# Block-sparse attention and a rational feed-forward layer on one core: the first two groups of input weights scaled and split through TensorE, loaded in pairs

## The chip, the core and the metric

One core of one Trainium2 chip runs the whole kernel. Time is device microseconds (us) for one execution. TensorE is PE in the profile, with its weight load PEld; VectorE is DVE, ScalarE is ACT, GpSimd is POOL, and SyncE, which issues most of the loads and stores, is SP.

## What is computed

Attention over blocks of 32 positions, 4 batches of 8 heads, 768 positions, 64 values per head; its output goes row by row through a feed-forward layer whose activation is a quotient of two polynomials. The feed-forward weights come as 64-bit floats.

```python
scores = scale * np.matmul(q, k.transpose(0, 1, 3, 2))
# kept: neighbouring blocks, first and last block, and 3 sampled blocks for each block of queries
scores = np.where(mask, scores, -1000000000.0)
attn = softmax(scores)
x = (attn @ v) as 3072 rows of 512

h = x @ w_in                      # 512 x 2048
P = a[0] + a[1] * h + a[2] * h**2 + a[3] * h**3
Q = 1.0 + abs(b[0]) * abs(h) + abs(b[1]) * h**2
out = (P / (Q + 1e-06)) @ w_out   # 2048 x 512
```

## The kernel before

The 3072 rows are 12 chunks of 256. For each chunk attention makes `x` (32 rows at a time, `attention`), splits it in two f16 parts `xh` and `xl`, and then eight **units** (`unit`, of 256 hidden values each) run: 24 matmuls into a PSUM tile `ph` (L1036 to L1038, `into`), three ScalarE passes and seven VectorE passes that make the quotient as `gh` (L1071) and its rest `gl` (L1081), and three groups of four matmuls into `acc` (L1093, L1095, L1099). The two `ph` buffers are one ring, `r_ph`.

Before the units can run, the weights have to be decoded (`weights`, L390 on). **w_in** is 4 column groups `u` of 512 columns, each of 4 row pieces `x` of 128 rows. A piece of 64-bit words (512 KB) is loaded into memory that `wo_l` and `wo_b` will use later. `convert` (L154 by DVE or POOL, L150 by ACT) scales the high word, and three VectorE operations L441, L444, L447 (`pack1` to `pack3`) shift and join the bits into a 32-bit float in place. `most` (L378, ACT) takes the largest absolute value of each piece. When the four pieces of a group are done, `w_scaled` finds one power of two for each group (`scales`: a transpose on TensorE, L339, and small VectorE operations L344 to L356, then L502), and for each piece runs three operations: `scaled` (L154, times the power of two, into a scratch tile `dw`, a ring of three), `high` (L150, to f16), and `low` (L519, POOL, the rest as f16). **w_out** is 16 pieces, each converted, packed and split in the same way into `wo_h`, `wo_l` and `wo_b`, with the same `dw` ring and a ring of two load buffers `wl`.

Each group's scale and the scale of the batch's `v` make the factors that the unit multiplies by (`factors`, L1010): four tiny VectorE operations for each group of the first batch, and four for each later batch.

What sets the order: nothing is issued as it is written. Every step is an `Op` with an engine (or a choice among engines, `among`), a price in ns, the steps it follows, a priority, and the ring buffers it takes. `issue` is a list scheduler that plays these forward and writes the instructions of every engine in the order it found. Where TensorE would idle early on, `fill` (L162) puts in matmuls of the identity whose result nobody reads. A step that may run on several engines goes to the one where it could start first, with the home engine preferred:

```python
key = (max(t - slack, now[e]) + (0 if e == o.engs[0] else other[e]), o.prio, o.n)
```

Of the kernel before, what the change touches and what calls it, by code (L numbers as in the profile page):

```python
# [11 lines left out]
F32 = mybir.dt.float32  # L12
# [3 lines left out]
I32 = mybir.dt.int32  # L16
# [8 lines left out]
def kernel(  # L25
# [68 lines left out]
    nc.vector.tensor_copy(out=ident16, in_=ident)  # L94

# [19 lines left out]
    class Op:  # L115


        def __init__(self, eng, price, run, after=(), prio=0.0, takes=(), uses=(), unit=None, behind=None):
# [9 lines left out]
            self.next, self.at, self.work = [], dict.fromkeys(self.engs, 0.0), 1.0  # L128
# [35 lines left out]
    def issue(ahead):  # L164
# [13 lines left out]
        busy, window, warm = {}, 0, False  # L178
        for n, o in enumerate(plan):
# [9 lines left out]
        fsh = 0.8  # L189
        other = {VE: 500, SC: 534.0, PO: 243.0}  # L190
        unit_of = {VE: nc.vector, SC: nc.scalar, PO: nc.gpsimd}
        slack, fend, f00, fgap = 21.0, 80000, 3000, 0
        while left:
# [53 lines left out]
            else:  # L247
                end = t = t + price
# [40 lines left out]
    absb = const.tile([P, 2], F32, name="absb")  # L289
    bias = const.tile([P, NB, NS], F32, name="bias")  # L290
# [6 lines left out]
    def setup():  # L297
        nc.vector.tensor_scalar(out=ix, in0=samp[0:1].rearrange("p i (n w) -> p i n w", w=2)[:, :, :, 0],
                                scalar1=0, scalar2=NB - 1, op0=ALU.max, op1=ALU.min)
        nc.scalar.activation(out=absb, in_=par[:, 4:6], func=AF.Abs)  # L300

# [66 lines left out]
    scrap = const.tile([P, 512], F16, name="scrap")  # L368
# [7 lines left out]
    def bound(src, mx):  # L376

        nc.scalar.activation(out=scrap[:, :src.free_size()], in_=src, func=AF.Abs, accum_out=mx)  # L378
# [18 lines left out]
    def weights():  # L397
# [5 lines left out]
        for u in range(NG):  # L403
            pieces += [(min(place[0, 2 * u], place[1, 2 * u]) + -4.91, 0, u, x) for x in range(NCC)]
# [5 lines left out]
        def raw(u, x):  # L410
            x0 = (x // 2 if u == 0 else 2 + x // 2) * NCC
            home = [wo_l, wo_b][x % 2][:, x0:x0 + NCC]
            return home.rearrange("p a n -> p (a n)").bitcast(I32)

        def homes(x):
            x //= NCC
            return [freed[0 if x < 2 else NG - 1, 2 * (x % 2) + y] for y in range(2)]

        def one(prio, kind, u, x, before):
# [4 lines left out]
            def load():  # L424
# [5 lines left out]
                if u == 0 and x == 0:  # L430
                    nc.gpsimd.tensor_copy(out=d["ld"][:, 0:1].bitcast(F32), in_=kall[:, 12, 0, 0:1])
                (nc.sync if u > 1 else nc.gpsimd).dma_start(out=d["ld"], in_=wi64[r0:r0 + P, u * 2 * WC:(u + 1) * 2 * WC])

            def convert(eng):
                d["w"] = early.tile([P, WC], I32, name="dw", bufs=3) if kind else wi[:, x, u].rearrange("p a n -> p (a n)").bitcast(I32)
                d["words"] = d["ld"].rearrange("p (n w) -> p n w", w=2)
                times(eng, d["w"].bitcast(F32), d["words"][:, :, 1].bitcast(F32), 2.0 ** -112)
# [5 lines left out]
            def pack2():  # L443
                nc.vector.scalar_tensor_tensor(out=d["w"], in0=d["words"][:, :, 0], scalar=29, in1=d["w"], op0=ALU.logical_shift_right, op1=ALU.bitwise_or)  # L444

            def pack3():
                nc.vector.scalar_tensor_tensor(out=d["w"], in0=d["words"][:, :, 1], scalar=-2 ** 31, in1=d["w"], op0=ALU.bitwise_and, op1=ALU.bitwise_or)  # L447

            def most():
                if u not in sums:  # L450
                    sums[u] = early.tile([P, 8], F32, name="sums")
                bound(d["w"].bitcast(F32), sums[u][:, x:x + 1])
# [9 lines left out]

            wl = [s_wl] if kind else []
            if kind or u > 1:
                o0 = Op(SY, [(475, 524288)], load, [o_setup] if kind else [freed[u - 1, x]], prio - 2, takes=wl, behind=before[kind])
            else:
                o0 = Op(PO, [(700, 524288)], load, [k_evac[0][3]] if u == 0 else [begun[0, x]], -17.0 + 1.2 * x if u else -84, behind=before[kind])
# [5 lines left out]
            o = Op(VE, 335, pack1, [o], prio, uses=w)  # L473
            o = Op(VE, 602, pack2, [o], prio, uses=wl + w)
            o = Op(VE, 602, pack3, [o], prio, uses=wl + w)
# [770 lines left out]
```

## Time and profile before

| what | value |
|---|---|
| median of 3 runs | 829.0 us (827.88 to 829.31) |
| profiled execution, its own time | 828.6 us |
| its span in the profile | 826.8 us |
| busy: PE, PEld, DVE, ACT, POOL | 770.6, 557.3, 674.9, 569.7, 107.5 us |
| instructions in the span | 27468 |
| POOL's last busy slice of 40 | slice 11 (all later ones are 0) |

The profiled execution's own time is 1.8 us over its span. A row of a view of instructions gives the start, the duration, engine, line and tiles; a group's row gives the total, the mean duration of one in ns and, behind the second bar, the idle time of the engine just before them with what ended it. The granted clock (PEclk) is a share of TensorE's full 2.4 GHz; 0.50 is the lower level, 1.2 GHz.

### The profile page before, as it was taken

How to read it: one execution, taken by the hardware profiler on the slowest of the kernel's cores; microseconds unless marked ns; L12 is line 12 of the kernel's file. 1: busy time of each engine (PE TensorE's matmuls, PEld its weight loads, DVE VectorE, ACT ScalarE, POOL GpSimd, SP SyncE). 2: the span in 40 equal slices, each digit the busy share in tenths (PEclk: the TensorE clock that was granted, in tenths of full speed). 3: DMA queues.
4: the chain of work that ended last, by engine and by line, in shares of the span. 5: the costliest groups of instructions: out<-in, count | busy, mean ns of one | idle time of the engine just before them, and what ended most of it. 6: DMA issues, size and time to landing. Idle time of an engine off the chain costs nothing.

```text
span 826.8 us, 27468 instructions
## 1 busy us (share of the span) xinstructions
PE 770.6 (93%) x10859; PEld 557.3 (67%) x10943; DVE 674.9 (82%) x1580; ACT 569.7 (69%) x1264; POOL 107.5 (13%) x149
## 2 busy tenths in 40 slices
PE   8798918898999999999999999999999999999997
PEld 4556605676677768677777767677777767767774
DVE  2788999899988885788878884887888886887886
ACT  2676777677866769677576759676676758766563
POOL 3547485613100000000000000000000000000000
PEclk9999969899999999999999999999999999999999
DMA  7988874537566957545636757635555436220000
GB/s 210 242 220 238 233 231 138 163 87 189 142 154 165 214 162 194 162 123 162 160 108 164 191 145 196 173 96 157 144 151 149 117 111 182 76 65 2 1 26 26
DMA packets 224416, 121.29 MB, mean 147 GB/s; under 512 B 62624, under 2 KB 214048, under 8 KB 224288
## 3 DMA queue, kind: packets, MB, share of 16 engines
q1 hardware_dynamic: 223136, 115.34, 51.6%
q0 software_dynamic: 1152, 4.19, 1.6%
q8 instruction: 86, 1.41, 0.8%
q14 instruction: 42, 0.34, 0.1%
HBM read 108.47 MB, written 11.01 MB: 145 GB/s over the span
## 4 chain that ended last, share of the span: by engine, by line
PE 81%; DVE 7%; DMA 4%; issue 3%; ACT 2%; POOL 2%; SPq 1%; ACTq 0%; POOLq 0%; DVEq 0%
PE acc L1093 11%; PE ph L1036 9%; PE acc L1095 9%; PE acc L1099 9%; PE ph L1037 9%; PE ph L1038 9%; PE m L817 7%; PE av L940 6%; PE m L894 6%; PE acc L162 3%; DMA vg<-in_v_dram 2%; PE m L556 2%; DMA wl<-in_moe_w_out_dram 1%; PE m L978 1%; POOL wo_h L154 1%
## 5 line engine op out<-in xcount | busy, mean ns | idle before, releaser
L1037 PE MATMUL ph<-xl,wi 128*128 128x256 f16 x768 | 210.5, 274 | 3.1 <-DVE xl L989 3.1
L1036 PE MATMUL ph<-xh,wi 128*128 128x256 f16 x768 | 210.9, 275 | 1.4 <-DVE tt L1053 1.4
L1038 PE MATMUL ph<-xh,wi 128*128 128x256 f16 x768 | 210.7, 274 | 0.0
L1043 ACT ACTIVATE sq<-ph,fc 128x512 f32<-128x512 f32 x96 | 65.9, 687 | 112.6 <-PE ph L1038 112.4
L1093 PE MATMUL acc<-wo_h,gh 128*128 128x512 f32 x384 | 114.5, 420 | 18.7 <-DVE gh L1071 18.0
L848 ACT ACTIVATE pr<-pr,st 128x256 f32<-128x256 f32 x224 | 110.7, 501 | 14.3 <-DVE st L860 14.3
L1060 DVE SCALAR_TENSOR_TENSOR ab<-sq,absb,ab 128x512 f32<-128x512 f32 x96 | 73.2, 763 | 37.1 <-ACT ab L1057 36.9
L829 DVE CUSTOM_DVE_ANT_1 pr<-m,bias 128x256 f32<-128x256 f32 x224 | 83.2, 418 | 22.3 <-PE m L817 22.1
L1099 PE MATMUL acc<-wo_b,gl 128*128 128x512 bf16 x368 | 95.4, 379 | 3.4 <-issue 2.1
L1095 PE MATMUL acc<-wo_l,gh 128*128 128x512 bf16 x316 | 86.5, 384 | 4.6
L1036 PEld LDWEIGHTS <-wi 128*128 128x128 f16 x768 | 75.9, 99 | 21.4 <-issue 5.1
L1071 DVE SCALAR_TENSOR_TENSOR gh<-tt,par,rr 128x512 fp32r<-128x512 f32 x96 | 72.3, 753 | 19.8 <-ACT rr L1067 11.2
L1093 PEld LDWEIGHTS acc<-wo_h,gh 128*128 128x128 f32 x384 | 66.0, 191 | 32.7 <-issue 19.6
L150 ACT ACTIVATE pT<-m 128x512 f32<-128x512 f32 x112 | 64.1, 596 | 34.0 <-PE m L894 32.7
L1037 PEld LDWEIGHTS <-wi 128*128 128x128 f16 x768 | 75.6, 98 | 12.7 <-issue 0.2
L1038 PEld LDWEIGHTS <-wi 128*128 128x128 f16 x768 | 75.5, 98 | 12.6 <-issue 3.4
L1047 ACT ACTIVATE tt<-ph,par,fc 128x512 f32<-128x512 f32 x96 | 74.8, 779 | 0.3 <-DVE gl L1081 0.2
L1050 DVE TENSOR_TENSOR tt<-tt,sq 128x512 f32<-128x512 f32 x96 | 66.9, 697 | 9.4 <-ACT tt L1047 9.4
L1057 ACT ACTIVATE ab<-ph,fc 128x512 f32<-128x512 f32 x96 | 65.6, 683 | 11.2 <-DVE tt L1077 10.5
L1077 DVE SCALAR_TENSOR_TENSOR tt<-tt,par,ab 128x512 f32<-128x512 f32 x96 | 72.2, 752 | 0.5
L894 PE MATMUL m<-ident,pr 128*128 128x128 f32 x448 | 69.6, 288 | 2.9 <-ACT kt L150 2.3
L1053 DVE SCALAR_TENSOR_TENSOR tt<-ph,fc,tt 128x512 f32<-128x512 f32 x96 | 71.4, 744 | 0.8
(130 smaller groups left out, 1221.7 us busy)
## 6 DMA issues: line engine op xcount, KB each, us to landing
vg<-in_v_dram SPq DMA_DIRECT2D x312, 64.0 KB, 2.9
vg<-in_v_dram SPq DMA_DIRECT2D x88, 192.0 KB, 3.6
kall<-ks SPq DMA_DIRECT2D x138, 64.0 KB, 1.9
wl<-in_moe_w_out_dram SPq DMA_DIRECT2D x16, 512.0 KB, 4.8
vg<-in_v_dram SPq DMA_DIRECT2D x12, 512.0 KB, 5.1
kall<-ks SPq DMA_DIRECT2D x23, 256.0 KB, 3.7
ldq<-in_q_dram SPq DMA_DIRECT2D x20, 256.0 KB, 3.4
out_dram<-ld SPq DMA_DIRECT2D x20, 256.0 KB, 2.4
```

The costliest lines, as they stand in the source:

```text
L829: nc.vector.tensor_tensor_reduce(out=prs[x][:, e, g].rearrange("p (s r) -> p s r", r=BLK), in0=h["sp"][g][:, e], in1=add.rearrange("p (s o ...
L848: nc.scalar.activation(out=prs[x][:, e, g], in_=prs[x][:, e, g], func=AF.Exp, scale=SCALE, bias=st[:, 12 + y:13 + y], accum_out=st[:, 16 + ...
L894: nc.tensor.transpose(pp[:, jj * P:(jj + 1) * P], pr[:, e, g, kt:NS * BLK:2], ident)
L1036: nc.tensor.matmul(o, wh, xh[:, :, cc], start=(cc == 0), stop=False)
L1037: nc.tensor.matmul(o, wh, xl[:, :, cc], start=False, stop=False)
L1038: nc.tensor.matmul(o, wl, xh[:, :, cc], start=False, stop=(cc == NCC - 1))
L1047: nc.scalar.activation(out=d["tt"], in_=d["ph"], func=AF.Identity, scale=d["cst"][:, 3:4], bias=par[:, 2:3])
L1060: nc.vector.scalar_tensor_tensor(out=d["ab"], in0=d["sq"], scalar=absb[:, 1:2], in1=d["ab"], op0=ALU.mult, op1=ALU.add)
L1071: nc.vector.scalar_tensor_tensor(out=d["gh"], in0=d["tt"], scalar=par[:, 0:1], in1=d["rr"], op0=ALU.add, op1=ALU.mult)
L1093: nc.tensor.matmul(acc, g, wo_h[:, f], start=(new and e == 0), stop=False)
L1095: nc.tensor.matmul(acc, g, wo_l[:, f], start=False, stop=False)
L1099: nc.tensor.matmul(acc, g, wo_b[:, f], start=False, stop=(last and e == 1))
```

## The change

- **Pairs.** A piece of w_in is now two of the former ones (1 MB for a load): 8 loads, conversions and bounds instead of 16, 24 packing operations instead of 48, each over twice the elements.
- **Groups 0 and 1 through TensorE.** Their scale is put on a diagonal matrix `dg` (one VectorE operation of 128x128 for each group). `whole` is a 32-bit matmul of `dg` with the piece into a `ph` buffer, `high` is ACT's copy of it to f16, `less` subtracts this f16 part in the same buffer by a matmul with a negated identity `minus16`, and `rest` is ACT's copy of what is left. Groups 2 and 3 keep the three operations as they were.
- **Factors.** One VectorE operation over a table of four coefficients (`coefs`, filled at the start) takes the place of four.
- **The scheduler** adds to VectorE's clock a share (`drag`) of the time for which certain POOL steps run beside it, and the prices of two POOL choices for w_out go up (`out_high` 588 to 1050, `out_low` 1225 to 1400).

```diff
-            pieces += [(min(place[0, 2 * u], place[1, 2 * u]) + -4.91, 0, u, x) for x in range(NCC)]
+            pieces += [(min(place[0, 2 * u], place[1, 2 * u]) + -4.91, 0, u, x) for x in range(0, NCC, 2)]
...
-            o = Op(among("c", SC, sc=520, po=588, ve=335), 0, convert, [o0], prio, takes=w, uses=wl)
+            o = Op(among("c", SC, sc=520, po=588, ve=335) if kind else among("c", SC, sc=890, po=1200, ve=602), 0, convert, [o0], prio, takes=w, uses=wl)
+            o.drag = 0.36
...
-                o1 = Op(among("o", SC, sc=520, po=588, ve=335), 0, out_high, [o], prio, uses=w)
-                o2 = Op(among("p", PO, po=1225, ve=602), 0, out_low, [o1] + homes(x), prio, uses=w)
+                o1 = Op(among("o", SC, sc=520, po=1050, ve=335), 0, out_high, [o], prio, uses=w)
+                o2 = Op(among("p", PO, po=1400, ve=602), 0, out_low, [o1] + homes(x), prio, uses=w)
+                o2.drag = 0.62
...
         def keep(s, inv):
+            if u < 2:
+                dg.append(p2.tile([P, P], F32, name="dg"))
+                nc.vector.tensor_scalar(out=dg[0], in0=ident, scalar1=s, scalar2=None, op0=ALU.mult)
...
+                def whole():
+                    d["w"] = ps_h.tile([P, 512], F32, name="ph")
+                    nc.tensor.matmul(d["w"], dg[0], wi[:, x, u].rearrange("p a n -> p (a n)").bitcast(F32), start=True, stop=True)
+
+                def less():
+                    nc.tensor.matmul(d["w"], minus16, wi[:, x, u, 0], start=False, stop=True, skip_group_check=True)
+
+                def rest():
+                    nc.scalar.activation(out=wi[:, x, u, 1], in_=d["w"], func=AF.Copy)
...
+                if u < 2:
+                    a = Op(TE, 880, whole, [o], prio, takes=[s_ws])
+                    a = Op(among("h", SC, sc=520), 0, high, [a], prio, uses=[s_ws])
+                    a = Op(TE, 230, less, [a], prio, uses=[s_ws])
+                    a = Op(SC, 520, rest, [a], prio, uses=[s_ws])
+                else:
+                    a = Op(among("s", PO, po=671, ve=396, sc=613), 0, scaled, [o], prio, takes=[s_ws])
+                    a.drag = 0.36
...
-            for j, coef in enumerate((1.0, absb[:, 0:1], par[:, 1:2], par[:, 3:4])):
-                nc.vector.tensor_scalar(out=fcs[b][:, j, u:u + n], in0=wscale[:, u:u + n], scalar1=v_inv[b], scalar2=coef, op0=ALU.mult, op1=ALU.mult)
+            nc.vector.scalar_tensor_tensor(out=fcs[b][:, :, u:u + n], in0=coefs.rearrange("p (j o) -> p j o", o=1).broadcast_to([P, 4, n]), scalar=v_inv[b],
+                                           in1=wscale[:, u:u + n].rearrange("p (o u) -> p o u", o=1).broadcast_to([P, 4, n]), op0=ALU.mult, op1=ALU.mult)
...
+                if e == PO and o.drag:
+                    while pooled and pooled[0][1] < t - 20000:
+                        pooled.pop(0)
+                    pooled.append((t, t + price, o.drag))
+                    late = o.drag * max(0.0, min(now[VE], t + price) - max(t, last_dve))
+                    now[VE] += late
+                if e == VE:
+                    last_dve = t
+                    price += dragged(t, price)
```

How the order moves, at two places. First VectorE between the scale of group 0 and the second half of chunk 0's `xl` (L1010 before, L1070 after, are the factors; `sums` is the largest value of group 1). Before:

```order
L502 COPY wscale<-scw 128x1 x2
L154 TENSOR_SCALAR dw<-wi,scw 128x512
L663 TENSOR_REDUCE mx<-mx 128x1
...
L660 COPY xscale<-sc_1035 128x1
L1010 TENSOR_SCALAR fc<-wscale,sc_1035 128x2
L1010 TENSOR_SCALAR fc<-wscale,sc_1035,absb 128x2
L1010 TENSOR_SCALAR fc<-wscale,sc_1035,par 128x2 x2
L498 TENSOR_REDUCE sums<-sums 128x1
```

and now:

```order
L721 COPY xscale<-sc_1013 128x1
L1070 SCALAR_TENSOR_TENSOR fc<-coefs,sc_1013,wscale 128x4x2
L535 TENSOR_REDUCE sums<-sums 128x1
L1050 SCALAR_TENSOR_TENSOR xl_120<-m_105,xscale,xh_119 128x512
L1027 TENSOR_TENSOR xn<-av,st 128x256
L468 TENSOR_SCALAR dw<-dw 128x512
L471 SCALAR_TENSOR_TENSOR dw<-wl,dw 128x512
L1050 SCALAR_TENSOR_TENSOR xl_120<-m_104,xscale,xh_119 128x512
L369 TENSOR_REDUCE scw<-m_105 128x1
```

The four factor operations are one, the scaling of a piece is gone from VectorE, `xl` stands directly behind the factors, and the scale of group 1 (`scw`), which stood ahead of the second `xl`, now stands behind it.

Second TensorE ahead of the first unit (L1001 is `av`, L556 here the new `whole`, L559 the new `less`, L164 the fills). Now:

```order
L1001 MATMUL av<-vg_114,pT 32x64 x16
L556 MATMUL ph<-wi,dg 128x512
L955 MATMUL m_104<-ident,pr 128x128 x4
L556 MATMUL ph<-wi,dg 128x512
...
L559 LDWEIGHTS minus_95
L559 MATMUL ph<-wi,minus_95 128x512
...
L556 MATMUL ph<-wi,dg 128x512 x2
L1039 MATMUL m_104<-ident,xn 128x128 x4
L559 LDWEIGHTS minus_95
L559 MATMUL ph<-wi,minus_95 128x512
```

None of these stood there before; fills did. Over the whole kernel the fills go from 135 to 121, and the two blocks of scores (L817) that stood ahead of the first unit's matmuls now stand behind them. From the 25th group of `acc` matmuls on, TensorE's order is the same before and after.

## Rows read from the trace of the kernel before

**Rows 1.** Busy time of the engines in stretches, with granted clock and DMA (columns first).

```profile
core 0: us, PE busy (x) PEld busy (x) DVE busy (x) ACT busy (x) POOL busy (x), PEclk, DMA share, GB/s
...
45.00:75.00 30.00, 27.80 (x574) 18.71 (x572) 27.00 (x75) 22.40 (x58) 20.37 (x27) 1.00 0.77 213
75.00:100.00 25.00, 20.48 (x350) 14.17 (x353) 21.25 (x63) 15.26 (x32) 11.18 (x17) 0.93 0.91 251
100.00:125.00 25.00, 7.38 (x35) 4.60 (x35) 23.23 (x41) 19.38 (x53) 18.77 (x10) 0.69 0.71 219
125.00:160.00 35.00, 27.95 (x583) 21.74 (x582) 32.26 (x73) 25.86 (x59) 23.70 (x28) 0.88 0.52 152
160.00:230.00 70.00, 65.87 (x935) 48.20 (x931) 69.77 (x157) 52.86 (x115) 15.91 (x15) 1.00 0.56 146
230.00:826.80 596.80, 583.60 (x7750) 426.44 (x7821) 476.51 (x1083) 412.88 (x896) 0.00 (x0) 1.00 0.48 130
```

**Rows 2.** What TensorE waited for, 45 to 160 us: total, times, longest.

```profile
PE acc L1093 <- DVE gh L1071: 18.0, 2, 17.6
```

**Rows 3.** Chain of work that ended last, 52 to 158 us: start, duration, what.

```profile
53.07 3.47 DVE fc L1010 x4
...
86.87 6.17 DMA wl<-in_moe_w_out_dram
...
101.42 7.89 POOL wo_h L154
```

**Rows 4.** Groups of VectorE instructions, 0 to 230 us, shapes apart.

```profile
L441 DVE TENSOR_SCALAR wi<-wi 128x512 int32<-128x512 int32 x16 | 7.5, 479 | 0.1
...
L444 DVE SCALAR_TENSOR_TENSOR wi<-wo_l,wi 128x512 int32<-128x512 int32 x8 | 5.5, 689 | 0.1
...
L154 DVE TENSOR_SCALAR dw<-wi,scw 128x512 f32<-128x512 f32 x4 | 4.9, 1239 | 3.4 <-POOL wi L519 2.0 <-POOL wo_l L461 1.4
L1010 DVE TENSOR_SCALAR fc<-wscale,sc,par 128x2 f32<-128x2 f32 x8 | 4.6, 613 | 0.0
...
L1010 DVE TENSOR_SCALAR fc<-wscale,sc 128x2 f32<-128x2 f32 x4 | 2.4, 603 | 0.0
...
L1010 DVE TENSOR_SCALAR fc<-wscale,sc,absb 128x2 f32<-128x2 f32 x4 | 2.0, 506 | 0.0
...
L347 DVE TENSOR_SCALAR scw<-scw 128x1 f32<-128x1 f32 x4 | 0.6, 142 | 0.0
...
L154 DVE TENSOR_SCALAR wi<-wo_b 128x512 f32<-128x512 f32 x1 | 0.4, 397 | 0.0
```

**Rows 5.** Timeline of VectorE, 61 to 73 us: start, duration, what.

```profile
61.99 1.21 DVE L444 SCALAR_TENSOR_TENSOR dw<-wl,dw 128x512 int32<-128x512 int32 x1
63.13 1.13 DVE L860 TENSOR_SCALAR st<-st 128x4 f32<-128x4 f32 x1
...
71.20 1.27 DVE L441 TENSOR_SCALAR dw<-dw 128x512 int32<-128x512 int32 x1
```

**Rows 6.** Groups of GpSimd instructions, 0 to 230 us.

```profile
L519 POOL TENSOR_TENSOR wi<-dw,wi 128x512 f16<-128x512 f32 x16 | 19.6, 1247 | 5.2 <-ACT wi L150 5.2
L154 POOL TENSOR_SCALAR wo_h<-dw 128x512 fp32r<-128x512 f32 x8 | 14.3, 1794 | 37.2 <-DVE dw L447 22.6 <-DVE st L872 8.7 <-DVE st L860 5.9
L154 POOL TENSOR_SCALAR dw<-wi,scw 128x512 f32<-128x512 f32 x12 | 9.6, 805 | 12.7 <-DVE scw L356 11.0 <-DVE wo_l L461 1.4
...
L154 POOL TENSOR_SCALAR wi<-wo_b 128x512 f32<-128x512 f32 x4 | 3.0, 753 | 0.0
```

**Rows 7.** One group of ScalarE instructions, 0 to 230 us.

```profile
L150 ACT ACTIVATE wi<-dw 128x512 f16<-128x512 f32 x16 | 9.8, 625 | 4.7 <-DVE dw L154 2.4 <-POOL dw L154 2.3
```

**Rows 8.** Groups of TensorE instructions, the whole span.

```profile
L1093 PE MATMUL acc<-wo_h,gh 128*128 128x512 f32 x384 | 114.5, 420 | 18.7 <-DVE gh L1071 18.0 <-ACT ld L150 0.7
...
L894 PE MATMUL m<-ident,pr 128*128 128x128 f32 x448 | 69.6, 288 | 2.9 <-ACT kt L150 2.3 <-ACT pT L150 0.6
```

**Rows 9.** Busy time of the fills (L162) alone, 45 to 75 us.

```profile
45.00:75.00 30.00, 12.07 (x51) 4.69 (x49) 1.00 0.77 213
```

More of the change, by code (lines that the diff above doesn't have):

```diff
@@ L94 @@
     nc.vector.tensor_copy(out=ident16, in_=ident)
+    minus16 = const.tile([P, P], F16, name="minus16")
+    nc.vector.tensor_scalar(out=minus16, in0=ident, scalar1=-1.0, scalar2=None, op0=ALU.mult)
     VE, SC, PO, TE, SY = "DVE", "Activation", "Pool", "PE", "SP"
@@ L127, in __init__ @@
                 s.left += 1
-            self.next, self.at, self.work = [], dict.fromkeys(self.engs, 0.0), 1.0
+            self.next, self.at, self.work, self.drag = [], dict.fromkeys(self.engs, 0.0), 1.0, 0.0
             plan.append(self)
@@ L178, in issue, with dragged @@
         busy, window, warm = {}, 0, False
+        pooled = []
+        def dragged(t, price):
+            more = 0.0
+            for a, b, drag in pooled:
+                more += drag * max(0.0, min(b, t + price) - max(a, t))
+            return more
         for n, o in enumerate(plan):
@@ L376, in bound @@
     def bound(src, mx):
-        nc.scalar.activation(out=scrap[:, :src.free_size()], in_=src, func=AF.Abs, accum_out=mx)
+        to = scrap[:, :src.free_size()]
+        nc.scalar.activation(out=to if len(src.shape) == 2 else to.rearrange("p (x n) -> p x n", x=2), in_=src, func=AF.Abs, accum_out=mx)
     kall = const.tile([P, NB, HG, BLK], F32, name="kall")
@@ L410, in raw @@
         def raw(u, x):
-            x0 = (x // 2 if u == 0 else 2 + x // 2) * NCC
-            home = [wo_l, wo_b][x % 2][:, x0:x0 + NCC]
-            return home.rearrange("p a n -> p (a n)").bitcast(I32)
+            x0 = 0 if u == 0 else 2 * NCC
+            home = [wo_l, wo_b][x // 2][:, x0:x0 + 2 * NCC]
+            return home.rearrange("p a n -> p (a n)").bitcast(I32).rearrange("p (x n) -> p x n", x=2)
         def homes(x):
             x //= NCC
-            return [freed[0 if x < 2 else NG - 1, 2 * (x % 2) + y] for y in range(2)]
+            return [freed[0 if x < 2 else NG - 1, 2 * y] for y in range(2)]
         def one(prio, kind, u, x, before):
@@ L430, in load @@
                 if u == 0 and x == 0:
[L431 to L432 removed]
+                    nc.gpsimd.tensor_copy(out=d["ld"][:, 0, 0:1].bitcast(F32), in_=kall[:, 12, 0, 0:1])
+                (nc.sync if u > 1 else nc.gpsimd).dma_start(out=d["ld"], in_=wi64[r0:r0 + 2 * P, u * 2 * WC:(u + 1) * 2 * WC].rearrange("(x p) n -> p x n", x=2))
             def convert(eng):
[L435 to L437 removed]
+                d["w"] = early.tile([P, WC], I32, name="dw", bufs=3) if kind else wi[:, x:x + 2, u].rearrange("p x a n -> p x (a n)").bitcast(I32)
+                lo, hi = [d["ld"].rearrange("p (n w) -> p n w" if kind else "p x (n w) -> p x n w", w=2)[(slice(None),) * (2 if kind else 3) + (w,)] for w in range(2)]
+                d["words"] = lo, hi
+                times(eng, d["w"].bitcast(F32), hi.bitcast(F32), 2.0 ** -112)
             def pack1():
@@ L485, in one @@
                 return o2
-            return Op(SC, 613, most, [o], prio)
+            return Op(SC, 980, most, [o], prio)
         group = []
@@ L519, in low @@
                     eng.tensor_tensor(out=wi[:, x, u, 1], in0=d["w"], in1=wi[:, x, u, 0], op=ALU.subtract)
-                a = Op(among("s", PO, po=671, ve=396, sc=613), 0, scaled, [o], prio, takes=[s_ws])
-                a = Op(among("h", SC, sc=520, po=588, ve=335), 0, high, [a], prio, uses=[s_ws])
-                a = Op(among("l", PO, po=1113, ve=602), 0, low, [a], prio, uses=[s_ws])
+                if u < 2:
[6 more added lines that the diff above has]
+                    a.drag = 0.36
+                    a = Op(among("h", SC, sc=520, po=588, ve=335), 0, high, [a], prio, uses=[s_ws])
+                    a = Op(among("l", PO, po=1113, ve=602), 0, low, [a], prio, uses=[s_ws])
+                    a.drag = 0.62
                 in_ready.setdefault(u, []).append(a)
```

40 lines of the change are left out of this document (27 added, 13 removed).

## The prediction, made before the changed kernel was run

> **What bounds the kernel now.** I read the table of stretches first. From 230 us to the end TensorE is busy for 583.6 of 596.8 us at a granted clock of 1.00, and from 160 to 230 for 65.9 of 70 [rows 1]: there it is the limit, and the change gives it the same matmuls in the same order from the 25th `acc` group on. What can move is how late this steady part begins. Between 45 and 160 us TensorE has holes, most of all from 100 to 125, where it is busy for 7.4 us and the granted clock falls to 0.69 of full speed [rows 1]. The list of waits names one for it: 17.6 us in which the third `acc` group waits for `gh` from VectorE [rows 2]. VectorE itself has no hole of that size: in the four stretches from 45 to 160 us it is busy for 27.0, 21.3, 23.2 and 32.3 us, 103.7 of 115 [rows 1]. So while the weights are decoded VectorE sets the pace, and TensorE later carries its delay to the end. The chain of waits shows what keeps VectorE there: the four factor operations take 3.47 us, a load of w_out is waited for 6.17 us, and one POOL copy takes 7.89 us [rows 3], against a mean of 1.79 for its group [rows 6].
>
> **The sum** is therefore made of VectorE's time between 45 and 160 us, against the profiled execution's 828.6 us (span 826.8 and 1.8 around it), which lies 0.4 under the median of 829.0.
>
> 1. *Factors.* The 16 operations of the first batch take 4.6 + 2.4 + 2.0 = 9.0 us [rows 4], although each handles two elements per partition. Four remain. One costs between 0.14 (the smallest VectorE operation) and 0.61 us (the old mean beside POOL) [rows 4], so 0.6 to 2.5 in all; I take 0.4 each, 1.6, between the two, since it still meets POOL. Gain 7.4 (6.5 to 8.4). The later batches' twelve operations lie where TensorE is the limit: nothing.
> 2. *Scaling of pieces.* VectorE did four of these at 1.24 us each and waited 1.4 us for POOL before one, because `dw` buffers were taken [rows 4]. By the order one remains, and groups 0 and 1 take no `dw` buffer: 3 x 1.24 + 1.4 = 5.1. Two `dg` operations of a quarter of the columns come in at 0.14 to 0.40 each [rows 4], 0.5 in all. Gain 4.6.
> 3. *POOL beside VectorE.* Eight `low` at 1.25 and six `scaled` at 0.81 us leave POOL, 14.8 us [rows 6]. Three VectorE instructions beside them took 1.21, 1.13 and 1.27 us [rows 5] where their like take 0.69, 0.14 and 0.48 [rows 4]: at most 2.3 comes back; at least nothing, since other POOL work may move up. I take 1.5.
> 4. *Pairs.* 48 packing operations become 24 of twice the elements. Joining two saves between nothing and the 0.14 of the smallest operation [rows 4]: 0 to 3.4; I take half, 1.7, and of that the half that belongs to groups 2 and 3, 0.8, because groups 0 and 1 are mostly packed before 45 us. The loads keep their bytes.
>
> Together 7.4 + 4.6 + 1.5 + 0.8 = 14.3 us less for VectorE.
>
> *What it costs elsewhere.* ScalarE gets eight copies more, at 0.63 us [rows 7] 5.0 us in a stretch where it is busy for 82.9 of 115 us [rows 1]; the bounds in pairs save some of it. I put it at zero; if ScalarE were late, the `ph` buffers would be (third rival). TensorE gets eight `whole` and eight `less`. A matmul of 512 columns takes 0.30 us in a 32-bit form and a 32-bit transpose of 128 columns 0.16, which makes 0.62 for 512 [rows 8]. `whole` lies between, and nearer to the second, whose operands are plain f32 too: 5.0 us, with eight `less` at 0.30 another 2.4. From 45 to 75 us TensorE spends 12.1 us on fills [rows 9] and 2.2 idle [rows 1], and 14 fills go: covered, zero.
>
> The Trainium skill (FP8 and Floating Point Precision, TensorE Precision Notes) says that true FP32 makes four passes through the array. No row here shows a plain f32 matmul of this width; an estimate by that page is 4 x 0.30 = 1.2 us for one `whole`, 9.6 for eight, and with `less` it would fill the 14.3 us of cover without going past it, so the sum would stay as it is and only the reserve would be gone.
>
> *What of it counts.* If only what the chain names counts, the first factors go from 3.47 to 0.4 and the 1.4 us wait goes: 4.5 us. If VectorE's whole saving reaches the end: 14.3. I take three quarters, 10.7: VectorE was busy for 90% of the stretch, which speaks for the upper end, but it will also meet loads (6.17 us on the chain) that come no earlier. 828.6 - 10.7 = 817.9 for the profiled execution, **818** for the median. POOL's 7.89 us I leave in: seven of the eight such copies stay on POOL. Late next is the same `gh`, behind the packing of w_out.
>
> **Rivals.**
>
> *Less than that.* VectorE and POOL hold each other up: the scaling of a piece takes VectorE 1.24 us in the stretches in which POOL works, a like operation without it 0.40 [rows 4]. The new POOL work is in longer pieces: the order has three conversions of pairs there, at 2 x 0.75 = 1.5 us each [rows 6], and each may hold VectorE for its whole length. For it: the POOL copy of 7.89 us [rows 3]. Against: POOL loses far more work than it gains in length. Then the gain is the chain's 4.5 less 3 x 0.75, some 2.2: 826.8. The Trainium skill (SBUF — State Buffer, Who interferes with whom) says that the shared port pair is locked for a whole instruction and the other engine blocks fully. By that rule the pairs cost VectorE what this rival says; the trace agrees in kind, with the 1.24 against 0.40 us.
>
> *More than that.* The 17.6 us wait shrinks so far that TensorE does not cool. From 100 to 160 us it ran 7.4 us at a clock of 0.69 and 28.0 at 0.88 [rows 1]; at full clock that is 2.3 + 3.4 = 5.7 less. With all of the 14.3: 829 - 20 = 809. Against: VectorE's list between the second and third `gh` is still long.
>
> *Slower.* A piece of groups 0 and 1 now holds one of the two `ph` buffers that the units need, until ScalarE has emptied it twice, and pieces of group 1 stand between the first unit's matmuls and the second's. ScalarE works in order, and the conversion of the first w_out piece, which waits for its load, stands among these copies. If that wait of 6.17 us [rows 3] lands on the buffers and the eight added copies (5.0) run one by one, 11.2 us are lost; with half of the 14.3 still won, the end is 4 us later: 833. It decides from the point where TensorE's idle time from 45 to 75 us, now 2.2, passes some 10 us. For it: the same two buffers serve both. Against: the first unit needs group 0 alone, and fills stood there before.
>
> That the drag does nothing is no rival of its own: my sum counts nothing for it.
>
> **How the numbers follow.** Forecast 0.60, with its own range of 812 (17.3 us, all upper bounds: 8.4 + 4.9 + 2.3 + 1.7) to 824.5 (4.5 us). Less 0.15, more 0.13, slower 0.12. A measurement of this kernel can tell 0.2%, 1.7 us, from no change. Below 827.3 lie the forecast, the larger gain and about half of the smaller: 0.81; within the bound 0.06; slower 0.13. The range reaches from 807 (the larger gain and 2 us) to 829 and leaves out the slower case and the far end of the larger one.
>
> **What would show it.** Right: TensorE's first unit starts about 5 us earlier than now; the factors take under 2.5 us in all; VectorE loses fewer than 3 us to waiting for POOL; the fifth `gh` comes some 10 us earlier; from there to the end the span is unchanged within 2 us. Wrong: the fifth `gh` no earlier (the work was not what held VectorE), a first unit later than now or a long idle time in 45 to 75 us (the buffers), or an early fifth `gh` and an unchanged end (TensorE was held by something else).

## The result, and the profile after

The change made the kernel slower: 834.1 us median (832.4 to 837.2) against 829.4 us (827.9 to 831.4) for the kernel before beside it, a ratio of 1.0061 with a 95% interval of 1.0045 to 1.0077, about 5 us. 818 was forecast, in a range that ended at 829. The profiled execution took 834.8 us, with a span of 832.9.

The stretches of the changed kernel, columns and cuts as in [rows 1] (the last ends with the span):

```profile
45.00:75.00 30.00, 29.27 (x504) 18.18 (x502) 22.93 (x75) 22.86 (x53) 8.91 (x18) 1.00 0.83 207
75.00:100.00 25.00, 21.89 (x452) 15.61 (x452) 19.64 (x47) 19.49 (x48) 11.50 (x17) 1.00 0.86 260
100.00:125.00 25.00, 15.24 (x111) 9.83 (x110) 24.90 (x52) 19.01 (x46) 10.10 (x8) 0.80 0.78 212
125.00:160.00 35.00, 27.04 (x493) 20.53 (x492) 33.13 (x62) 24.63 (x49) 20.28 (x21) 0.95 0.50 144
160.00:230.00 70.00, 60.90 (x914) 43.96 (x913) 63.97 (x141) 52.78 (x116) 20.36 (x21) 0.98 0.64 160
230.00:832.90 602.90, 596.05 (x7925) 431.27 (x7923) 481.24 (x1088) 418.47 (x910) 0.00 (x0) 1.00 0.54 129
```

Much of what was forecast is here. TensorE is busy for 15.2 us from 100 to 125 us instead of 7.4, at a granted clock of 0.80 instead of 0.69; POOL has less than half the work from 45 to 75. Yet from 160 to 230 us TensorE is busy for 60.9 us instead of 65.9, and what follows 230 us takes 602.9 us instead of 596.8. The 17.6 us wait for the third `gh` [rows 2] is gone. What TensorE waits for now, 45 to 160 us:

```profile
PE m L955 <- ACT kt L152: 9.1, 1, 9.1
PE m L955 <- ACT ab L1118: 5.2, 1, 5.2
```

VectorE's operations, 0 to 230 us, against [rows 4], and the two new kinds of matmul, 40 to 130 us (of TensorE's matmuls a 32-bit one may stand as two records: the 16 are eight instructions):

```profile
L1070 DVE SCALAR_TENSOR_TENSOR fc<-coefs,sc,wscale 128x8 f32<-128x8 f32 x4 | 1.0, 255 | 0.0
L542 DVE TENSOR_SCALAR dg<-ident,scw 128x128 f32<-128x128 f32 x2 | 0.6, 278 | 0.0
L156 DVE TENSOR_SCALAR dw<-wi,scw 128x512 f32<-128x512 f32 x1 | 1.5, 1482 | 0.0
...
L556 PE MATMUL ph<-wi,dg 128*128 128x512 f32 x16 | 8.3, 618 | 0.0
L559 PE MATMUL ph<-wi,minus 128*128 128x512 f16 x8 | 3.0, 379 | 0.0
```

The factors fell from 9.0 to 1.0 us. VectorE did save time: up to the start of the 28th `acc` group, behind which both kernels take as long (483.3 and 483.6 us), it is busy for 278.6 us instead of 288.1. Before and after (columns as in [rows 1], cut at that start):

```profile
0.00:343.50 343.50, 298.29 (x4702) 212.83 (x4726) 288.09 (x709) 239.10 (x556) 107.51 (x149) 0.96 0.70 188
```

```profile
0.00:349.30 349.30, 306.20 (x4736) 214.29 (x4736) 278.63 (x670) 242.37 (x548) 85.12 (x128) 0.97 0.75 184
```

That is 9.5 us less. The forecast was 14.3, of which 1.4 was waiting, so 12.9 of work. Some of the difference is in operations that the change didn't touch. Two of the units' operations, 0 to 230 us, before and after, and the first of them after 230 us, where POOL is idle:

```profile
L1050 DVE TENSOR_TENSOR tt<-tt,sq 128x512 f32<-128x512 f32 x15 | 11.5, 766 | 0.0
L1081 DVE TENSOR_TENSOR gl<-tt,rr 128x512 bf16<-128x512 f32 x14 | 10.3, 734 | 0.0
```

```profile
L1111 DVE TENSOR_TENSOR tt<-tt,sq 128x512 f32<-128x512 f32 x14 | 13.6, 972 | 0.0
L1142 DVE TENSOR_TENSOR gl<-tt,rr 128x512 bf16<-128x512 f32 x12 | 11.7, 972 | 0.1
```

```profile
L1111 DVE TENSOR_TENSOR tt<-tt,sq 128x512 f32<-128x512 f32 x82 | 56.2, 686 | 9.2 <-ACT tt L1108 9.2
```

So VectorE did less work, if not as much less as forecast, and the end moved the other way. The next table shows where; its times are starts on TensorE, read from the timelines of the profiled executions (the kernels e5 to e14 are those of the experiments below). Each row is one execution; e7, in the changed kernel's order and as slow, lies up to 1.8 us from that kernel's row, so differences of that size mean little.

| us | first scores | third `acc` group | 5th | 10th | 14th | 28th |
|---|---|---|---|---|---|---|
| before | 19.2 | 122.1 | 160.1 | 194.8 | 229.7 | 343.5 |
| after | 22.1 | 122.4 | 158.2 | 194.6 | 235.9 | 349.3 |
| e5, before with tiles 32 bytes on | 21.4 | 127.1 | 164.8 | 199.4 | 234.0 | 347.5 |
| e6, after with targets realigned | 19.4 | 118.9 | 156.0 | 192.4 | 232.0 | 345.8 |
| e9, factors in the old order | 19.5 | 122.8 | 159.7 | 194.3 | 228.6 | 342.0 |
| e14, third `gh` moved | 19.5 | 106.8 | 159.0 | 193.4 | 228.0 | 341.4 |

The changed kernel is 3 us late at the first scores, ahead of everything that the change meant to touch; it is level at the tenth group, and 6 us late at the fourteenth.

### The profile page after: what moved, and what is told of

Same layout as the page of the kernel before. It is cut to its first block, busy times and chain, and to the rows that moved or that the text cites. A ratio compares the mean times of both kernels' runs of the same rounds, so it can differ in the third digit from the quotient of the medians.

```text
span 832.9 us, 27466 instructions
## 1 busy us (share of the span) xinstructions
PE 784.0 (94%) x10953; PEld 558.9 (67%) x10953; DVE 664.6 (80%) x1535; ACT 573.2 (69%) x1256; POOL 85.1 (10%) x128
## 4 chain that ended last, share of the span: by engine, by line
PE 83%; DVE 6%; DMA 4%; SPq 3%; issue 2%; ACT 2%; POOL 0%; ACTq 0%; DVEq 0%
PE acc L1154 11%; PE acc L1156 10%; PE acc L1160 10%; PE ph L1097 9%; PE ph L1099 9%; PE ph L1098 9%; PE m L878 7%; PE av L1001 6%; PE m L955 6%; PE acc L164 2%; PE m L617 2%; PE m L1039 1%; DMA ldq<-in_q_dram 1%; DMA vg<-in_v_dram 1%; DMA kall<-ks 1%
## 5 line engine op out<-in xcount | busy, mean ns | idle before, releaser
L1121 DVE SCALAR_TENSOR_TENSOR ab<-sq,absb,ab 128x512 f32<-128x512 f32 x96 | 75.8, 789 | 37.9 <-ACT ab L1118 37.7
L1160 PE MATMUL acc<-wo_b,gl 128*128 128x512 bf16 x384 | 98.8, 380 | 3.1 <-DVE gl L1142 3.1
L1156 PE MATMUL acc<-wo_l,gh 128*128 128x512 bf16 x384 | 100.3, 384 | 0.0
L955 PEld LDWEIGHTS m<-ident,pr 128*128 128x128 f32 x448 | 63.4, 207 | 24.0 <-ACT kt L152 9.6
L1111 DVE TENSOR_TENSOR tt<-tt,sq 128x512 f32<-128x512 f32 x96 | 69.8, 727 | 9.2 <-ACT tt L1108 9.2
```

Of the source, the lines that this page charges most:

```text
L955: nc.tensor.transpose(pp[:, jj * P:(jj + 1) * P], pr[:, e, g, kt:NS * BLK:2], ident)
L1121: nc.vector.scalar_tensor_tensor(out=d["ab"], in0=d["sq"], scalar=absb[:, 1:2], in1=d["ab"], op0=ALU.mult, op1=ALU.add)
L1156: nc.tensor.matmul(acc, g, wo_l[:, f], start=False, stop=False)
L1160: nc.tensor.matmul(acc, g, wo_b[:, f], start=False, stop=(last and e == 1))
```

## The experiments

All medians below are in us, each with the kernel before measured beside it.

| run | median | before | ratio and interval |
|---|---|---|---|
| e1_last_load | 835.0 | 830.0 | 1.0063 (1.0045 to 1.0081) |
| e2_factors_only | 835.0 | 830.0 | 1.0059 (1.0040 to 1.0079) |
| e3_no_pairs | 838.6 | 830.0 | 1.0100 (1.0071 to 1.0129) |
| e4_no_split | 838.1 | 830.0 | 1.0100 (1.0069 to 1.0132) |
| e5_before_shift32 | 836.2 | 829.6 | 1.0074 (1.0057 to 1.0090) |
| e6_after_pad224 | 831.6 | 829.6 | 1.0018 (1.0004 to 1.0031) |
| e7_after_pad32 | 834.1 | 829.6 | 1.0056 (1.0030 to 1.0082) |
| e8_factors_pad224 | 829.4 | 829.6 | 0.9988 (0.9975 to 1.0002) |
| e9_factors_old_order | 827.9 | 830.3 | 0.9975 (0.9958 to 0.9992) |
| e10_no_pairs_pad224 | 831.2 | 830.3 | 1.0013 (0.9994 to 1.0033) |
| e11_no_split_pad224 | 831.6 | 830.3 | 1.0029 (1.0010 to 1.0048) |
| e12_no_drag_pad224 | 829.4 | 830.3 | 0.9993 (0.9978 to 1.0008) |
| e13_before_all256 | 829.3 | 829.3 | 0.9999 (0.9983 to 1.0014) |
| e14_third_gh | 827.5 | 829.3 | 0.9979 (0.9965 to 0.9994) |
| e15_no_pack2 | 824.9 | 829.3 | 0.9943 (0.9923 to 0.9963) |
| e16_last_load_pad224 | 830.1 | 829.3 | 1.0008 (0.9991 to 1.0025) |
| e17_before_shift64 | 834.4 | 829.7 | 1.0063 (1.0042 to 1.0084) |
| e18_before_shift128 | 833.8 | 829.7 | 1.0052 (1.0032 to 1.0072) |

### First theories: one load, or one part of the change

**e1_last_load.** The scheduler's order was written out as a list and played back, with one entry moved:

```diff
 SP:  L980 DMA vg <- v
+SP:  L453 DMA wl <- w_out
 SP:  L836, L838, L842 DMA kall <- ks
-SP:  L453 DMA wl <- w_out
```

> Every engine's order is that of the changed kernel, instruction by instruction, but for one: the load of the last piece of w_out stands on SP ahead of the k loads of a block (L836 to L842) instead of behind them. Theory A (this place in SP's order is the late loss): the load is issued at about 204 us instead of 210, the second half of the eighth-to-last decode stall (PE 4.9 of 10 us busy from 210 to 220 us) closes, and the time falls by 4 to 6 us, from 834 to 828 to 830. Theory B (VectorE or the early loads set the end, and the stall at 210 us only shows where the delay surfaces): less than 1.5 us, 833 or more.

Theory A fell: 1.0063 against 1.0061. In the changed kernel's chain of work that ended last, 200 to 222 us, the load is the longest piece (start, duration, what):

```profile
209.97 4.89 DMA wl<-in_moe_w_out_dram
```

SyncE's timeline of the changed kernel, and then of e1:

```profile
209.97 0.36 SPq L453 DMA_DIRECT2D wl<-in_moe_w_out_dram  x1
```

```profile
206.44 0.36 SPq L453 DMA_DIRECT2D wl<-in_moe_w_out_dram  x1
```

The load came 3.5 us earlier, and TensorE's scores still started at 220.8 us (219.5 without the move), because VectorE went through its list without a break before it. The chain of e1 that ended last, near its end:

```profile
217.94 0.60 DVE dw L471
218.54 0.66 DVE tt L1138
219.20 0.60 DVE dw L474
219.80 0.60 DVE gl L1142
220.41 0.33 DVE pr L890
...
220.80 1.24 PE m L878 x37
```

The chain before showed the load as the wait that ended last; taking it away showed the next one, as late.

**e2_factors_only, e3_no_pairs, e4_no_split.** Each takes a part alone, or takes one out:

```diff
 e2, in the kernel before:
-            for j, coef in enumerate((1.0, absb[:, 0:1], par[:, 1:2], par[:, 3:4])):
-                nc.vector.tensor_scalar(...)
+            nc.vector.scalar_tensor_tensor(...)
 e3, in the changed kernel:
-            pieces += [... for x in range(0, NCC, 2)]
+            pieces += [... for x in range(NCC)]
 e4, in the changed kernel:
-                if u < 2:
+                if u < 0:
```

> The kernel before with one part of the change: the factors as one VectorE operation over the table of coefficients, at its new price in the scheduler. The prediction's term 1 says 7.4 us of VectorE's time go, of which three quarters would reach the end: 829.4 - 5.5 = about 824. Theory B (VectorE's time before 160 us isn't what sets the end, the order found by the scheduler is): anything from 826 to 834, with the fifth gh less than 2 us earlier.

> The changed kernel with w_in loaded and packed one piece at a time, as before; TensorE's split, the factors and the drag stay. If the 1 MB loads and the doubled operations cost the early 3 to 7 us (the scores of blocks 3 and 4 late), the scores of block 3 are back at about 31 us instead of 36.8 and the time is 828 or less. If the start is late for another reason, the fourth score block stays near 41 us and the time stays above 832.

> The changed kernel with groups 0 and 1 scaled and split by VectorE, ScalarE and POOL, as before; pairs, factors and drag stay. If the split through TensorE holds the ph buffers and ScalarE (the prediction's rival slower), taking it out gives 829 or less. If the split is free or saves VectorE's time, the time stays at 834 or rises to 838, with the 17.6 us wait for the third gh back at over 12 us.

None is faster than the whole change. e2, at 835.0, lies just above the 826 to 834 of its theory B. e3 fell on the second of its cases, above 832: its third score block starts at 36.7 us (36.8 in the changed kernel, 30.6 before), so pairs are not what delays it. e4, at 838.1, is where its second case put it, but the wait for the third `gh`, which should have come back to over 12 us, is under 1. What they have in common with the changed kernel is the first 20 us, and there e2 has neither pairs nor a split nor drag. The only thing left was the table `coefs` itself.

### The table moves the tiles behind it

`coefs` holds 16 bytes per partition and takes 32; `minus16` takes 256, and `scrap` grew by 1024. Together every tile allocated later begins 1312 = 5 x 256 + 32 bytes further on. The targets of the k, q and v loads (`tt`, `ab`, `sq`, `ldq`, `vg`, most of `ld`) began at multiples of 256 bytes before, `vg` at 114688, and begin 32 bytes past one now, at 116000. (Some later buffers of `ld` lay 64 bytes past one before and lie 96 past now; the target `wl` of the w_out loads went from 128 to 160.)

The DMA issues before 12 us (KB each, median us from issue to landing), in the kernel before and then in the changed one:

```profile
tt<-in_k_dram SPq DMA_DIRECT2D x2, 256.0 KB, 4.1
ab<-in_k_dram SPq DMA_DIRECT2D x2, 256.0 KB, 4.3
sq<-in_k_dram SPq DMA_DIRECT2D x2, 256.0 KB, 4.1
ldq<-in_q_dram SPq DMA_DIRECT2D x1, 256.0 KB, 4.3
```

```profile
tt<-in_k_dram SPq DMA_DIRECT2D x2, 256.0 KB, 4.6
ab<-in_k_dram SPq DMA_DIRECT2D x2, 256.0 KB, 5.3
sq<-in_k_dram SPq DMA_DIRECT2D x2, 256.0 KB, 5.2
ldq<-in_q_dram SPq DMA_DIRECT2D x1, 256.0 KB, 5.9
```

These are the same loads, ahead of any load of weights.

**e5_before_shift32, e6_after_pad224, e7_after_pad32, e8_factors_pad224.** The edit is the same line with a different width (8 words in e5 and e7, 56 in e6 and e8):

```diff
-    wscale = const.tile([P, NU], F32, name="wscale")
+    wscale = const.tile([P, NU], F32, name="wscale"); pad = const.tile([P, 8], F32, name="pad")
```

> The kernel before with nothing changed but an unused tile of 32 bytes per partition behind wscale, so that every tile allocated after it (vg, ldq, tt, ab, sq, ld, wl, kt) begins 32 bytes later: at 32 instead of 0 past a multiple of 256 bytes for the targets of the k, q and v loads. The order of every engine is the same. Theory C (the table coefs of the change moved these tiles by 32 bytes and the loads into them became slower): the k loads before 10 us fall from 288 to about 219 GB/s, the start is 3 us later, and the time rises from 829.4 to between 833 and 837. Theory D (the changed and the partly changed kernels are slow because the scheduler found other orders): no change, 829 to 830.

> The changed kernel with an unused tile of 224 bytes per partition behind wscale: vg, ldq, tt, ab, sq and ld begin at multiples of 256 bytes again, as in the kernel before; nothing else differs and the order of every engine is the same. Theory C: the start of 12.1 us for the q transposes comes back, the 10 us that PE lost before 45 us shrink by 3 or more, and the time falls by 5 to 12 us, to between 822 and 829; by the prediction's own sum it would be 818. Theory D: no change, 834.

> The changed kernel with an unused tile of 32 bytes per partition behind wscale: the targets of the loads begin 64 bytes past a multiple of 256. If being off 64 bytes is what slows the loads, it is as fast as the version with 224 bytes. If being off 256 bytes is, it stays at 834. [...]

> The kernel before with the factors as one operation and the same 224 bytes behind wscale. Theory C with the prediction's term 1: the loads are as fast as before the change and 7.4 us of VectorE's time are gone, of which three quarters would reach the end: about 824. If VectorE's time before 160 us isn't what sets the end: 829 to 830. Theory D: 835, as without the 224 bytes.

Theory C held for the loads, and D fell; but e6 got back 3.6 us where C said 5 to 12. With 32 idle bytes and no instruction changed, the kernel before is slower by 0.74%, 6 us, about as much as the whole change cost. The stretch from 6 to 11 us (columns as in rows 1, the last GB/s) in the kernel before, in e5, and in e6:

```profile
6.00:11.00 5.00, 4.81 (x18) 3.34 (x19) 2.86 (x19) 1.19 (x2) 0.00 (x0) 1.00 1.15 261
```

```profile
6.00:11.00 5.00, 3.95 (x17) 2.55 (x18) 2.84 (x18) 1.20 (x2) 0.00 (x0) 0.70 1.35 218
```

```profile
6.00:11.00 5.00, 4.82 (x18) 3.29 (x19) 3.93 (x25) 1.19 (x2) 0.00 (x0) 1.00 1.04 236
```

In e5 the DMA engines are busier (1.35 against 1.15) and move less. With aligned targets this stretch has lulls, so the rates are better compared where the loads come without a break, from 6 to 7 us, in the kernel before and in the changed one:

```profile
6.00:7.00 1.00, 0.81 (x4) 0.71 (x5) 0.86 (x6) 0.00 (x0) 0.00 (x0) 1.00 1.23 279
```

```profile
6.00:7.00 1.00, 0.45 (x4) 0.42 (x4) 0.90 (x7) 0.00 (x0) 0.00 (x0) 1.00 1.38 218
```

It isn't only the start. From 235 to 780 us the 64 KB loads of v, rows of 512 bytes, land later too (median us to landing, in the kernel before and in e5):

```profile
vg<-in_v_dram SPq DMA_DIRECT2D x208, 64.0 KB, 2.8
```

```profile
vg<-in_v_dram SPq DMA_DIRECT2D x208, 64.0 KB, 3.7
```

In e6 it is 2.9 us and in the changed kernel 3.7. Behind the 28th group this hardly counts: from there to the end e5 takes 484.1 us and the kernel before 483.3.

e6 has the early landings back (4.1 to 4.6 us for k) and, with the lowest DMA share of the three, moves more than e5. The first unit starts at 61.5 us in e6, against 65.9 both before and after the change (67.9 in e13, in the order of before). The changed kernel gets back 0.43% (1.0061 to 1.0018), 3.6 us, and the factors alone 0.71%. 64 bytes off (e7) gives nothing back.

**e17_before_shift64, e18_before_shift128.** The same line with 16 and 32 words, in the kernel before:

> The kernel before with an unused tile of 64 bytes per partition behind wscale, order unchanged: the targets of the k, q and v loads begin 64 past a multiple of 256. If any start off 256 splits the 256-byte rows of these loads, the k loads run at about 219 GB/s and the time is 833 to 837, as with 32 bytes. If 64 is enough, 829 to 830.

> The same with 128 bytes: the targets begin 128 past a multiple of 256. If any start off 256 splits the rows, 833 to 837; if 128 is enough, 829 to 830.

Both are slower than the kernel before, by 0.63% and 0.52%. The same stretch in e17 and in e18:

```profile
6.00:11.00 5.00, 4.46 (x17) 3.09 (x18) 2.80 (x18) 1.11 (x2) 0.00 (x0) 1.00 1.34 218
```

```profile
6.00:11.00 5.00, 4.32 (x17) 3.06 (x18) 3.05 (x19) 0.97 (x2) 0.00 (x0) 1.00 1.28 218
```

32, 64 and 128 bytes off give the same 218 GB/s. Of the offsets tried, 0, 32, 64 and 128, only 0 escapes it.

**e13_before_all256** aligns `kall` and w_in's targets, which were off 256 in the kernel before, too (`wl` and some of `ld` stay off):

```diff
-    scrap = const.tile([P, 512], F16, name="scrap")
+    scrap = const.tile([P, 512], F16, name="scrap"); pad0 = const.tile([P, 8], F32, name="pad0")
...
-    wscale = const.tile([P, NU], F32, name="wscale")
+    wscale = const.tile([P, NU], F32, name="wscale"); pad = const.tile([P, 56], F32, name="pad")
```

> The kernel before with unused tiles ahead of kall and behind wscale, so that kall, the targets of w_in and all later load targets begin at multiples of 256 bytes (kall and w_in's targets were 224 past one); the order and the instructions are the same. If the factors gave e9 its 2 us, this one is at 829 to 830.5, as the kernel before; if the alignment of kall did, it is at 827 to 828.5.

0.9999: no gain. These two kinds of targets take 512 bytes and 4 KB in a row where the k and q loads take 256. `kall`'s 64 KB loads land in 1.9 us in both kernels (235 to 780 us): its rows are as long as those of v, but a load of `kall` spreads over 128 partitions and one of v over 16. Why the one is slowed and not the other is open. It is also the control for the next run.

### Why the saved work brings so little

**e9_factors_old_order.** The kernel before, aligned, with one factor operation where four stood, and the old order played back (otherwise as e8):

> The kernel before with the factors as one operation and the load targets at multiples of 256 bytes, and with the order of all instructions kept as in the kernel before: each factor operation stands where its four stood. Theory E (the saved VectorE time is real, but the list scheduler, given the lower price, found an order that wastes it): here it reaches the end, and the time is 3 to 7 us below before, 823 to 827, against 829.4 with the scheduler's own order. Theory F (VectorE's time for the factors isn't on the path that sets the end): 828.5 to 830 in this order too.

0.9975, 2.1 us: between the ranges of the two theories, in neither. With e13 at 0.9999 it comes from the factors. In the scheduler's own order (e8) 0.12% was left, so the reordering took up to half of it, though the intervals overlap. VectorE's factors in e9, 0 to 230 us:

```profile
L1014 DVE SCALAR_TENSOR_TENSOR fc<-coefs,sc,wscale 128x8 f32<-128x8 f32 x4 | 2.1, 520 | 0.0
```

So 9.0 - 2.1 = 6.9 us of operations went from VectorE and 2.1 reached the end: 30%, with a wide margin, since the interval of e9 alone reaches from 0.7 to 3.5 us.

**e15_no_pack2.** In e9's kernel and order:

```diff
             def pack2():
+                if not kind: return
                 nc.vector.scalar_tensor_tensor(...)
```

> The kernel of e9 without the second packing operation of w_in: 16 operations of about 0.69 us, 11 us of VectorE's time before 160 us, with the order of everything else kept. It leaves out the low words' bits of w_in. If VectorE's amount of work set the end as the prediction had it (three quarters of what it saves), 8 us: about 820. If the chain runs from engine to engine and VectorE only waits longer: 825 to 828.

0.9943 against 0.9975 for e9: 0.32%, 2.7 us, for the 11.5 us that the 16 operations took in e9. That is 23%, just past the edge of the second case. Both steps together take 18.4 us of operations away and bring 0.57% (0.37 to 0.77), 4.7 us: a quarter, with 17 to 35% as its interval. Where the rest went can be seen up to the 28th group, in e9 and in e15:

```profile
0.00:342.00 342.00, 300.72 (x4726) 213.44 (x4726) 284.00 (x698) 239.26 (x556) 100.41 (x149) 0.96 0.70 189
```

```profile
0.00:339.70 339.70, 295.72 (x4702) 211.47 (x4726) 274.29 (x682) 238.62 (x556) 97.72 (x149) 0.96 0.69 190
```

VectorE is busy for 9.7 us less (the operations left take 1.8 us more), its idle time grows from 58.0 to 65.4, and the group starts 2.3 us earlier.

**e14_third_gh.** In e9's kernel eight entries of the order move ahead (VectorE; `ab`, `tt`, `gh`, `gl` are the third unit's, `wi` the packing of later groups):

```diff
+L1065 SCALAR_TENSOR_TENSOR ab<-sq,absb,ab
+L1058 SCALAR_TENSOR_TENSOR tt<-ph,fc,tt
 L452 SCALAR_TENSOR_TENSOR wi<-wo_l,wi
+L1076 SCALAR_TENSOR_TENSOR gh<-tt,par,rr
 L446 TENSOR_SCALAR wi<-wi x2
...
-L1076 SCALAR_TENSOR_TENSOR gh<-tt,par,rr
```

> The kernel of e9 with eight operations moved: the third unit's denominator, cubic, gh and gl on VectorE and its Ln and Exp on ScalarE stand ahead of the packing of groups 2 and 3 of w_in and not behind it. Theory G (VectorE's order sets the end): the third acc group starts at about 110 us instead of 122.8, the wait of 16.6 us is cut by 10 or more, and the time falls by 3 to 10 us, to between 818 and 825. Theory H (the wait is cover for what comes later anyway, the attention blocks and the pieces of w_in): the wait moves to the next unit, and the time is 826 to 829.

Theory H held. What TensorE waited for in e9, 45 to 235 us, and in e14, 100 to 125 us:

```profile
PE acc L1098 <- DVE gh L1076: 17.2, 2, 16.6
```

```profile
PE m L899 <- ACT kt L150: 13.9, 1, 13.9
PE acc L1098 <- DVE gh L1076: 4.5, 1, 4.5
```

The third group starts 16 us earlier, at 106.8, and the next matmul then waits 13.9 us for a copy that stands on ScalarE behind the next unit's Ln and Exp, which waited for VectorE. The fourth group is 1.0 us earlier, and the end is where it was (0.9979 and 0.9975). The longest wait of the profile was cover for what came later anyway. This tests VectorE's order and not the amount of its work: from 100 to 122 us it is busy for 21.9 of 22 us in e14. The amount is what e15 tests.

**e10_no_pairs_pad224, e11_no_split_pad224, e12_no_drag_pad224.** The edits of e3 and e4, and one that turns the drag and the new prices off, each with the 224 bytes:

```diff
-                if e == PO and o.drag:
+                if False:
...
-po=1050, po=1400
+po=588, po=1225
```

> The changed kernel with the load targets at multiples of 256 bytes, and w_in one piece at a time. It was 4.5 us slower than the changed kernel without the 224 bytes; if the pairs save work, it is at 834 to 836 here, against 831.6 with them. If their price was another order only, anything between 828 and 836.

> The changed kernel with the load targets at multiples of 256 bytes, and groups 0 and 1 scaled and split without TensorE. By the prediction's terms 2 and 3 the split is worth 4.6 + 1.5 us of VectorE's time: 834 to 837, against 831.6 with it. By its rival (ph buffers and ScalarE): below 831.

> The changed kernel with the load targets at multiples of 256 bytes, and with the scheduler as before: no drag, and 588 and 1225 as POOL's prices. The instructions are the same, the order is another. The prediction counted nothing for this: 831 to 833. If orders alone move the time by several us, it may lie at 826 or at 838.

Without pairs 1.0013 and without the split 1.0029 can't be told from e6's 1.0018; the 4 us that each seemed to cost in e3 and e4 didn't come again. Both expectations of a loss missed, and no single part is shown to gain or to lose. Without the drag it is 0.9993: 2.1 us better than with it, by the middles, with intervals that just overlap. The order is another, and so are some choices of engine (POOL has 133 operations and ScalarE 1250, against 128 and 1256 in e6). Up to the 28th group of e12:

```profile
0.00:344.90 344.90, 306.48 (x4730) 214.78 (x4731) 273.48 (x671) 237.81 (x542) 90.75 (x133) 0.97 0.69 187
```

VectorE is busy for 14.6 us less than in the kernel before, more than the sum forecast, and the time is 0.6 us shorter, from 1.8 shorter to 0.7 longer. In this order hardly any of it reaches the end.

**e16_last_load_pad224** repeats e1 on aligned tiles:

> The changed kernel with aligned load targets and the last load of w_out ahead of a block's k loads on SP. VectorE had 2.1 us idle of the five from 210 to 215 us there: if the load sets it, the time falls by about 2, to 829 to 830; if VectorE's order does, as in the unaligned pair, it stays at 831 to 832.

1.0008 against 1.0018: in the expected direction, and not to be told apart. What the late loss would have been worth stays open.

## Why the prediction was wrong

The sign was missed, and the range with it. Two steps failed, and a third was half right.

*"The loads keep their bytes."* This put the loads at nothing. The bytes stayed and their targets moved. The sum had no term for a tile of 16 bytes in the diff, though the list of allocations stood in the kernel. In the order of before the move costs 6 us (e5); in the changed order putting it right gives 3.6 back (e6), of a loss of 5. This made most of the loss. It did not alone decide the sign: aligned, the change is at 1.0018 (1.0004 to 1.0031) and still brings no gain.

*"What of it counts ... I take three quarters."* This was a size, and a large one: 10.7 us. About a quarter of the VectorE time that was taken away reached the end in the order of before (e9, e15), and next to nothing in an order of the changed kernel's own (e12: 14.6 us less work, 0.6 us gained). Being busy for 90% of a stretch did not mean that VectorE set the end: each engine goes through its list in a fixed order and waits for the others in turn, and an engine that is done sooner waits longer (e15: 9.7 us less work, 7.4 us more idle time). e14 shows that the 17.6 us wait, on which the argument rested, was worth nothing by itself.

*The 14.3 us of VectorE.* Of the 12.9 us of work in it 9.5 came. The factors gave 8.0 us (7.4 forecast), the packing of w_in fell from 30.8 to 27.5 us, and two `dg` operations took 0.6 (0.5). Term 3 came out the other way. POOL did lose work (107.5 to 85.1 us), and the packing of w_out, which is VectorE's work beside it, fell from 36.5 to 30.5 us; but the units' operations grew, the two shown above and `ab` (841 to 1027 ns) by some 8 us together.

By the quarter, an estimate from e9 and e15, 9.5 us would be some 2.4 at the end. The new order seems to have used them up: the aligned change is at 1.0018 with the drag and 0.9993 without. "That the drag does nothing is no rival of its own" is therefore doubtful, though the difference of 2.1 us is not settled.

The other steps: the first unit "about 5 us earlier" came out as 4.3 once the loads were right (e6), and as nothing in the changed kernel, where the late start hid it. The fifth `acc` group was 1.9 us earlier and not 10 (4.1 in e6). "From there to the end the span is unchanged" failed as well: it is 8.0 us longer (674.7 against 666.7), lost ahead of the 28th group. The cause of that part is not shown: e1 ruled out the late load for the changed kernel, and e16 left it open for the aligned one. `whole` took 8.3 / 8 = 1.04 us and not the 0.62 of the sum. The Trainium skill (FP8 and Floating Point Precision, TensorE Precision Notes), from whose four passes the estimate of 1.2 was made, was nearer. Fills did go for it (135 to 121), and TensorE's idle time from 45 to 75 us did not grow.

The rivals: *slower* had the sign and not the cause. TensorE's idle time from 45 to 75 us fell from 2.2 to 0.7 us instead of passing 10, so by its own sign the `ph` buffers held nothing up. (The first `acc` group does start later, at 99.6 us instead of 89.8, and at 94.5 in e11, without the split; why is not shown, and at the third group before and after are level again.) *Less* named POOL's conversions of pairs, which took 1.4 and 1.1 us; VectorE's waits for POOL before 230 us fell from 5.4 to 2.4 us (its start-up wait of 1.4 left out). What it said of the two engines holding each other up shows in the longer unit operations; it takes from the saving and doesn't explain a loss. *More* saw rightly that the granted clock from 100 to 125 us would rise (0.69 to 0.80), but this did not reach the end either.

## What to carry to other kernels

Read the allocations of a diff as carefully as its instructions: a small new tile can move every later one, and transfers with short rows then change their speed. Look at the first transfers, ahead of anything that the change touches, and compare their landing times before explaining later stages. And before a saving on a busy engine is counted, find what share reaches the end, by taking some of its work away with the order kept; here it was a quarter in one order and nothing that could be measured in another, and the longest wait was worth nothing.

## What the runs showed of the hardware

Loads with rows of 256 bytes into targets that begin 32, 64 or 128 bytes past a multiple of 256 ran at 218 GB/s from 6 to 11 us, all three alike; aligned ones, in the kernel before, moved 261 in that stretch and 279 in its first microsecond, and landed in 4.1 to 4.3 us instead of 4.6 to 5.3. Loads of 64 KB with rows of 512 bytes, 16 partitions each, landed in 3.7 us off by 32 and in 2.8 aligned (`vg`); those over 128 partitions landed in 1.9 off by 224 and aligned (`kall`), and aligning `kall` and w_in's targets made no difference to the time that could be measured (e13).

The Trainium skill (DMA: Bandwidth & Descriptors, How a descriptor splits into AXI transactions) says that a transaction must start at a multiple of 256 bytes, and that a descriptor which does not start at one begins with a transaction from the boundary below it; it tells this of reads. By that rule a row of 256 bytes takes two transactions instead of one, whatever the offset, and by the page's beats of 32 bytes nine, ten and twelve beats instead of eight for offsets of 32, 64 and 128. From the 279 GB/s above the beats alone give an estimate of 248, 223 and 186 GB/s. The three measured rates are alike at 218, here for writes into SBUF: that goes with the count of transactions and not with the beats. The runs don't show a transaction as such.

The aligned versions, each with an order of its own from the list scheduler (e6, e8, e10, e11, e12), lie between 0.9988 and 1.0029, 1 us below to 2.4 us above the kernel before; they differ a little in their work too, so what the order alone is worth isn't shown. The fastest kernels that compute everything, e9 and e14, keep the order of before (e14 but for eight entries) and are faster than both kernels, by 0.2% over the one before.
